# Sliding-window attention and a gated MLP on one core: some transposes of x moved from TensorE to DMA

## The chip, the core and the metric

The kernel runs on one NeuronCore of a Trainium2 chip. A core has TensorE (PE in the profile, with its weight loads as PEld), VectorE (DVE), ScalarE (ACT), GpSimd (POOL), SyncE (SP) and 16 DMA engines. Here SP and POOL do little more than issue DMAs. The metric is the device time of one execution in microseconds; lower is better. Executions differ by about half a per cent.

## What is computed

Eight batches of eight heads go through causal attention with a window of 128 and a distance penalty per head. The result, 4608 tokens of 512 features, goes through a two-layer MLP with the activation h cos h.

```python
scores = scale * np.matmul(q, k.transpose(0, 1, 3, 2))          # q, k, v: 8 x 8 x 576 x 64
mask = (rel >= 0) & (rel < window)                              # window = 128
scores = np.where(mask, scores + bias[None], -1000000000.0)     # bias = -slope_h * |rel|
attn = softmax(scores)
x = np.matmul(attn, v)            # to 4608 x 512
h = x @ w_in                      # 512 x 2048
g = h * np.cos(h)
out = g @ w_out                   # 2048 x 512
```

## The kernel before

**Units and chunks.** Attention is cut into 64 units. A batch has eight: one for its first 128 queries and all heads (`qb` 0, "first unit"), six for 128 queries and half of the heads each (`qb` 1 to 3, "half-width units"), and one for its last 64 queries and all heads (`qb` 4, "tail unit"). The MLP is cut into nine chunks of 512 tokens. The first projection of chunk c (`moe1`, line 731; line 756 for chunk 0) makes 16 blocks of 128 features, 4 matmuls each; ACT takes the cosine of each block (line 736) and DVE multiplies (line 740) into `gT`, of which there are two. The second projection (`moe2`, line 784) has 64 matmuls per chunk, whose results go through `ob` (four buffers) to HBM by a store on SP (line 796).

**Phases.** Seven units are done in a startup phase. Then follows, for each chunk c, `moe1` of c, an exp phase c with eight units (nine in phase 6), and `moe2` of c. Phases exist because ACT holds one function table at a time (exp or sine). The eight units of phase c are the tail of batch c, then the first unit and the six half-width units of batch c + 1. They are handled in pairs: scores of both units (line 541), two exps (line 568), masks on DVE (line 587), the product with v (PV, lines 603 to 617) and the normalization (lines 640 to 656), which leaves x with tokens on partitions in `xtail`, `xfirst` or `xnat`. Scores use the four PSUM banks `SB`; PV uses the two banks `UB`. A half-width unit takes one bank of `UB`, so both units of a pair fit; a first or tail unit takes both.

**Transposes of x.** `moe1` needs x with features on partitions (`xT`). Function `x_pe` (line 661) does this with PE transposes into the free part of the unit's `UB` banks (line 675 for first and tail units, four each; line 694 for half-width units, two each) and copies out of PSUM by ACT or DVE (lines 703, 704: two copies for a first unit, one for any other). Function `x_dma` (line 708) does it with one DMA transpose from SBUF to SBUF, issued on SP (line 718, and 714 for first and tail units). Line 826 chooses `x_dma` only for units that do not begin in the chunk that comes next.

**Transposes of q and k.** From batch 2 on, POOL loads q and k with a cast to `qnat` and `knat` (line 380), and SP turns them into `qt` and `kt` by DMA transposes (lines 389 and 392, two issues each). `qnat` and `knat` have one buffer each, so the next load waits until the transposes have read them. `qt` and `kt` have two buffers by parity of the batch: those of batch c + 2 can be written once the scores of the tail of batch c, in the first pair of phase c, are done, and are read by the first pair of phase c + 1. POOL issues in program order: v of the next batch, then q and k.

**Order of the work.** Class `Plan` records every operation with an estimated occupancy (`occ`) and latency (`lat`) and derives dependencies from what it reads and writes. `schedule` is a list scheduler over these estimates: at each step it takes the earliest operation, on PE by priority (PV 1, scores 2, `moe1` 5, `moe2` 6; lower first). It fixes the order of every engine's instructions and of SP's issues. At run time each engine goes through its list in that order and waits on semaphores. Lines 170 to 178 estimate when a DMA ends; line 165 doubles PE's occupancies before `COLD`.

Of the kernel before, what the change touches and what calls it, by code (L numbers as in the profile page):

```python
# [12 lines left out]
NPAIR = H // 2  # L13
# [5 lines left out]
CH = 512  # L19
# [15 lines left out]
class Plan:  # L35
# [3 lines left out]
    SWITCH = 110  # L39
    TABLE = 1330  # L40
    START = {"pe": 1300, "act": 750, "dve": 1050, "pool": 550, "sp": 750}
    COLD = 8000
    FILL = 107

    def __init__(self, nc, ctx):
# [2 lines left out]
        self.writer, self.readers = {}, {}  # L48
        self.lastdma, self.lastseq = {}, {}

    def op(self, eng, fn, r=(), w=(), dma=None, occ=100, lat=None, pri=5, mode=0, table=None):
        o = Op()
        o.seq = len(self.all)
        o.eng = (eng,) if isinstance(eng, str) else tuple(eng)
        o.fn, o.r, o.w, o.dma = fn, tuple(r), tuple(w), dma
        o.occ, o.lat, o.pri, o.mode, o.table = occ, occ if lat is None else lat, pri, mode, table
        preds = {}
        for k in o.r:
            if k in self.writer:
                preds[self.writer[k]] = DATA  # L60
        for k in o.w:
            if k in self.writer:
                preds[self.writer[k]] = DATA
            for d in self.readers.get(k, ()):
                preds.setdefault(d, WAR)
        if dma is not None and dma in self.lastdma:
            preds[self.lastdma[dma]] = DATA
        if eng == "pool":
            if eng in self.lastseq:
                preds.setdefault(self.lastseq[eng], ORDER)  # L70
            self.lastseq[eng] = o
        if dma is not None:
            self.lastdma[dma] = o
        o.preds, o.succs, o.npred = preds, [], len(preds)
        for d in preds:
            d.succs.append(o)
        for k in o.r:
            self.readers.setdefault(k, []).append(o)
        for k in o.w:
            self.writer[k], self.readers[k] = o, []  # L80
        self.all.append(o)
        return o
# [7 lines left out]
    def schedule(self, filler=None, fill=(0, 0)):  # L90
# [32 lines left out]
        while avail:  # L123
            phase = next((t for t in tables if left[t]), None)
            best = None
            for e in ENG:
                cand = []
                for o in avail:
                    if e not in o.eng or (o.table is not None and o.table != phase):
                        continue  # L130
                    at = reach(o, e)
                    st = max(free[e], at)
                    if e == "pe":
                        if o.mode != mode:
                            st += self.SWITCH
                        if at > free[e]:
                            st += 40
                    cand.append((st, o))
                if not cand:
                    continue  # L140
                if e == "pe":
                    st, o = pick_pe(cand)
                else:
                    soon = min(st for st, _ in cand)
                    st, o = min(((st, o) for st, o in cand if st <= soon + 40),
                                key=lambda c: (c[1].pri, c[1].seq))
                key = (st, o.pri, o.seq)
                if best is None or key < best[0]:
                    best = (key, e, o)
            (st, _, _), e, o = best  # L150
            avail.remove(o)
            if o.table is not None and o.table != table:
                st += self.TABLE
            if len(o.eng) > 1:
                o.fn, o.occ, o.lat = o.fn[e], o.occ[e], o.lat[e]
                o.eng = (e,)
            if e == "pe":
                while filler and mode == 0 and free[e] + self.FILL + 30 < st and (
                        fill[0] <= free[e] < fill[1]):
                    p = self.op("pe", filler, r=["zeros"], occ=self.FILL, lat=self.FILL + 100)  # L160
                    self.all.pop()
                    p.start, p.end = free[e], free[e] + self.FILL
                    free[e] += self.FILL
                    order.append(p)
                if st < self.COLD:
                    o.lat += o.occ
                    o.occ *= 2
            o.start = st
            free[e] = st + o.occ
            if o.dma is not None:  # L170
                if e == "sp" and o.dma[0] in "tx":
                    cross = max(cross, st + 2300) + o.lat
                    o.end = max(cross, st + o.occ + 1400) + 500
                elif e == "sp" and o.dma[0] == "s":
                    o.end = st + o.occ + 1800 + o.lat
                else:
                    wire = max(wire, st + (2300 if e == "pool" else 1400)) + o.lat
                    o.end = max(wire, st + o.occ + 1400) + 500
            else:
                o.end = st + o.lat  # L180
            if e == "pe":
                mode = o.mode
            if o.table is not None:
                table = o.table
                left[o.table] -= 1
            order.append(o)
            for s in o.succs:
                s.npred -= 1
                if s.npred == 0:
                    avail.append(s)  # L190
# [85 lines left out]
def bass_alibi_sliding__then__act_gcu_kernel(  # L276
# [8 lines left out]
    with ExitStack() as ctx:  # L285
# [96 lines left out]
                    src[b, :, 128 * t:128 * t + rows, :].rearrange("h p d -> p h d")))  # L382
            op("pool", fns, w=[("nat", which)], dma=f"ldn{which}", occ=4400, lat=5500)

        def dma_transposes(b):
            for which in ("q", "k"):
                t = tr[which][b % 2][:, :].rearrange("p (c k t) -> p c k t", c=NBLK, k=NPAIR)
                fns = [
                    lambda e, t=t, which=which: e.dma_start_transpose(
                        t[:, 0:4, :, :].rearrange("p c k t -> p (c k) t"),  # L390
                        nat[which][:, 0:4, :, :].rearrange("p c h d -> p (c h d)")),
                    lambda e, t=t, which=which: e.dma_start_transpose(
                        t[:, 4, :, 0:64],
                        nat[which][0:64, 4, :, :].rearrange("p h d -> p (h d)")),
                ]
                op("sp", fns, r=[("nat", which)] + ([("ktail", b % 2)] if which == "k" else []),
                   w=[("tr", which, b % 2)], dma=f"tr{which}{b % 2}", occ=2500, lat=6500)

        def load_w_in(f0, f1):
            op("pool", [lambda e: e.dma_start(  # L400
# [118 lines left out]
        def t_first(u):  # L519
            return S * u[0] + 128 * u[1]  # L520
# [185 lines left out]
                   occ={"act": 281, "dve": 320}, lat={"act": 384, "dve": 405}, pri=0)  # L706

        def x_dma(u, n):
            b, qb, hh = u
            t0 = t_first(u)  # L710
            if qb in (0, 4):
                m = 64 if qb else 128
                src_, key = (xtl[b % 2], ("xtl", b % 2)) if qb else (xfirst, "xfirst")
                op("sp", [lambda e: e.dma_start_transpose(xT[:, :, t0:t0 + m], src_[:, :])],
                   r=[key], w=xkeys(range(NPAIR), t0, m), dma=f"xt{b % 2}" if qb else "xf",
                   occ=1250, lat=500)
                return
            op("sp", [lambda e: e.dma_start_transpose(
                xT[:, 2 * hh:2 * hh + 2, t0:t0 + 128], xnat[n % NX][:, :])],
               r=[("xnat", n % NX)], w=xkeys(range(2 * hh, 2 * hh + 2), t0, 128), dma=f"x{n % NX}",  # L720
               occ=1250, lat=500)
# [78 lines left out]
        ucount = [0]  # L800

        def attention(us, phase):
            for g in range(0, len(us), 2):
                two = us[g:g + 2]
                if phase < 0:
# [13 lines left out]
                for set_ in sets:  # L819
                    pv(set_)  # L820
                    after = []
                    for u, ub in set_:
                        n = ucount[0]
                        ucount[0] += 1
                        norm(u, ub, n)
                        after.append((t_first(u) // CH > phase + 1, u, ub, n))
                    for by_dma, u, ub, n in after:
                        if by_dma:
                            x_dma(u, n)
                        else:  # L830
                            x_pe(u, ub, n)

        load_qk("q", q, 0, 0)
        load_qk("k", k, 0, 0)
# [28 lines left out]
        for c in range(NCH):  # L863
# [13 lines left out]
                    moe1(c, fc, (UB + SB)[fc % 6] if done < len(every) else  # L877
                         (UB + SB)[(16 * c + fc) % 6])
            n = QUOTA[c] if c < len(QUOTA) else 0
            attention(every[done:done + n], c)  # L880
            done += n
            while next_v < B and done >= 8 * (next_v - 1):
                load_v(next_v)
# [1 line left out]
            while next_t < B and done >= 8 * (next_t - 1):  # L885
                if next_t < 4:
                    tail_zero(next_t)
                dma_transposes(next_t)
                next_t += 1
                if next_t < B:  # L890
                    load_nat("q", q, next_t)
                    load_nat("k", k, next_t)
# [32 lines left out]
```

## Time and profile before

| what | value |
|---|---|
| median of 3 runs | 320.49 us (320.01 to 321.6) |
| profiled execution, its own time | 321.72 us |
| its span in the profile | 320.0 us |
| granted TensorE clock, mean | 0.994 |
| transposes of x on PE (lines 675 and 694) | 108 |
| DMA transposes into `xT` (lines 714 and 718) | 25 |
| DMA transposes of q and k (lines 389 and 392) | 24 |

The profile is of one execution. Its page gives the busy time of each engine and the chain of work that ended last, followed back from the end. In the rows of the timeline the columns are start in us, duration in us, engine, line, operation, what is written and read, shape and count; a bracket holds the idle time of the engine before the row and what ended it. Rows of one kind that follow each other are merged. A row for SPq is the issue of a DMA by SP, not its transfer. Matmuls are pipelined, so their durations overlap; the distance between starts is what one costs. A few per cent of the matmul records are missing; the weight loads (PEld) are counted in full. A row of a table by stretches gives the stretch, its length, then for each engine busy time and count, the granted TensorE clock, the mean number of busy DMA packets per DMA engine, and GB/s.

### The profile page before, as it was taken

Reading aid. Unit: us, or ns where it says so; the run is one execution under the profiler, and the core shown is the slowest. Engines: PE = TensorE matmul, PEld = TensorE weight load, DVE = VectorE, ACT = ScalarE, POOL = GpSimd, SP = SyncE. Lnnn points to the kernel's source line nnn. Section 1 sums busy time; section 2 is a strip of 40 time slices with the busy share of each in tenths; the row PEclk is TensorE's granted clock in tenths of the full one; section 3 lists DMA queues with packets and bytes.
Section 4 is the critical chain, followed back from the end, with each engine's and each line's share of the span. In section 5 each row is a group of like instructions: output and inputs, shape, how many; then the busy total and the mean of one; then the engine's idle time right before and its main releaser. Section 6 shows DMA issues by size and latency. Waiting matters only on the chain.

```text
span 320.0 us, 6788 instructions
## 1 busy us (share of the span) xinstructions
PE 307.2 (96%) x2741; PEld 163.0 (51%) x2781; DVE 196.9 (62%) x424; ACT 203.4 (64%) x277; POOL 96.6 (30%) x124
## 2 busy tenths in 40 slices
PE   7499999999999999999999999999999999999996
PEld 4379855444554554445445544554455444444444
DVE  6289858486868686859785877766578542263000
ACT  6498767686778676866687768567668643263111
POOL 8789340084491076107613570100000000000000
PEclk9799999999999999999999999999999999999999
DMA  7999999999999399949998997971011200201112
GB/s 120 167 204 206 206 164 190 164 148 159 164 200 109 74 158 160 97 104 121 173 107 125 196 136 53 158 137 25 33 68 28 65 3 33 96 5 66 66 68 98
DMA packets 141663, 37.22 MB, mean 116 GB/s; under 512 B 130240, under 2 KB 136640, under 8 KB 141632
## 3 DMA queue, kind: packets, MB, share of 16 engines
q0 software_dynamic: 100144, 18.10, 76.8%
q1 hardware_dynamic: 41488, 18.69, 27.0%
q8 instruction: 22, 0.36, 0.5%
q14 instruction: 9, 0.07, 0.1%
HBM read 36.70 MB, written 9.44 MB: 144 GB/s over the span
## 4 chain that ended last, share of the span: by engine, by line
PE 90%; ACT 3%; DMA 2%; issue 2%; POOL 1%; DVE 1%; ACTq 0%; POOLq 0%
PE ps L784 39%; PE ps L731 32%; PE ps L541 5%; PE ps L756 4%; DMA qrows<-in_q_dram 2%; PE ps L615 2%; PE ps L617 2%; ACT p L568 2%; PE ps L483 1%; PE ps L675 1%; PE ps L603 1%; PE ps L694 1%; DVE gT L740 1%; ACT cos L736 1%; PE ps L607 1%
## 5 line engine op out<-in xcount | busy, mean ns | idle before, releaser
L784 PE MATMUL ps<-w_outb,gT 128*128 128x512 bf16 (+2 forms) x566 | 133.2, 373 | 2.4 <-issue 1.6
L731 PE MATMUL ps<-xT,w_inb 128*128 128x512 bf16 x499 | 113.2, 379 | 0.7
L740 DVE TENSOR_TENSOR gT<-ps,cos 128x512 bf16<-128x512 f32 x128 | 83.6, 687 | 45.8 <-PE ps L784 28.6
L736 ACT ACTIVATE cos<-ps,halfpi 128x512 f32<-128x512 f32 x128 | 83.2, 687 | 31.6 <-PE ps L731 16.6
L784 PEld LDWEIGHTS ps<-w_outb,gT 128*128 128x128 bf16 x592 | 53.5, 98 | 55.4
L568 ACT ACTIVATE p<-ps 128x1024 bf16<-128x1024 f32 x64 | 62.0, 1021 | 30.4 <-PE ps L541 30.3
L731 PEld LDWEIGHTS ps<-xT,w_inb 128*128 128x128 bf16 x512 | 48.9, 98 | 59.1 <-DVE gT L740 3.5
L370 POOL DMA_DIRECT2D vp<-in_v_dram x40 | 34.0, 880 | 68.4 <-PE ps L607 60.2
L587 DVE TENSOR_TENSOR p<-p,emask 128x1024 bf16<-128x1024 bf16 x61 | 41.0, 684 | 6.4 <-ACT p L568 6.2
L791 ACT ACTIVATE ob<-ps 128x512 f32<-128x512 f32 (+2 forms) x25 | 14.5, 581 | 36.8 <-PE ps L784 36.8
L380 POOL DMA_DIRECT2D qnat<-in_q_dram x30 | 25.3, 886 | 21.2 <-DMA qt<-qnat 21.2
L380 POOL DMA_DIRECT2D knat<-in_k_dram x30 | 25.4, 884 | 13.5 <-DMA kt<-knat 12.8
L541 PE MATMUL ps<-qt,kt 64*128 64x128 bf16 (+1 forms) x576 | 20.8, 212 | 0.4 <-ACT kt L497 0.4
L541 PEld LDWEIGHTS ps<-qt,kt 64*128 64x128 bf16 x576 | 14.7, 95 | 7.7 <-issue 3.2
L654 DVE TENSOR_TENSOR xnat<-ps,rec 128x256 bf16<-128x256 f32 x48 | 18.3, 419 | 0.1
L756 PE MATMUL ps<-xT,w_inb 128*128 128x128 bf16 x256 | 16.8, 219 | 0.2 <-DVE rec L652 0.2
L615 PEld LDWEIGHTS ps<-vp,p 128*128 128x128 bf16 x192 | 12.7, 97 | 7.2 <-issue 6.4
L615 PE MATMUL ps<-vp,p 128*128 128x65 bf16 x192 | 15.2, 193 | 0.3
L617 PE MATMUL ps<-vp,p 128*128 128x65 bf16 x192 | 15.2, 193 | 0.0
L756 PEld LDWEIGHTS ps<-xT,w_inb 128*128 128x128 bf16 x256 | 14.5, 98 | 0.9 <-issue 0.3
L792 DVE COPY ob<-ps 128x512 f32<-128x512 f32 x12 | 8.3, 688 | 9.3 <-PE ps L784 9.2
L617 PEld LDWEIGHTS ps<-vp,p 128*128 128x128 bf16 x192 | 12.5, 97 | 0.0
(63 smaller groups left out, 173.3 us busy)
## 6 DMA issues: line engine op xcount, KB each, us to landing
out_dram<-ob SPq DMA_DIRECT2D x35, 256.0 KB, 2.3
vp<-in_v_dram POOLq DMA_DIRECT2D x32, 128.0 KB, 6.9
qnat<-in_q_dram POOLq DMA_DIRECT2D x24, 128.0 KB, 7.0
knat<-in_k_dram POOLq DMA_DIRECT2D x24, 128.0 KB, 6.3
w_outb<-in_moe_w_out_dram POOLq DMA_DIRECT2D x4, 512.0 KB, 19.8
w_inb<-in_moe_w_in_dram POOLq DMA_DIRECT2D x3, 512.0 KB, 13.0
qrows<-in_q_dram POOLq DMA_DIRECT2D x1, 576.0 KB, 12.8
krows<-in_k_dram POOLq DMA_DIRECT2D x1, 576.0 KB, 15.6
```

The source lines that it names most:

```text
L370: op("pool", [lambda e, t=t, rows=rows: e.dma_start(vp[b % 2][0:rows, t, :, 0:64], v[b, :, 128 * t:128 * t + rows, :].rearrange("h p d -> ...
L380: fns.append(lambda e, t=t, rows=rows: e.dma_start(nat[which][0:rows, t, :, :], src[b, :, 128 * t:128 * t + rows, :].rearrange("h p d -> p ...
L541: ins = e.matmul(ps[:, banks[x], c0:c0 + n_], keys_ap(b, x, pr, kc), query_ap(b, x, pr, qb, n_), start=not acc, stop=stop)
L568: op("act", lambda e: e.activation(P[i][:, 0:1024], ps[:, banks[0]:banks[0] + 2, :].rearrange("p a b -> p (a b)"), ACTF.Exp, scale=0.125), ...
L587: op("dve", lambda e: e.tensor_tensor(p, p, m, ALU.mult), r=[("P", i), ("EM", 0), ("EM", 1)], w=[("P", i)], occ=600, lat=690, pri=1)
L615: e.matmul(o, P[i][:, c0:c0 + 128], V[:, qb - 1, h, 0:65], start=True, stop=False)
L617: ins = e.matmul(o, P[i][:, c0 + 128:c0 + 256], V[:, qb, h, 0:65], start=False, stop=True)
L731: op("pe", lambda e, kc=kc: e.matmul(ps[:, bank, :], w_in[:, kc, 128 * fc:128 * fc + 128], xT[:, kc, r0:r0 + CH], start=(kc == 0), stop=(k ...
L736: op("act", lambda e: e.activation(cosb[ci][:, :], ps[:, bank, :], ACTF.Sin, bias=halfpi[:, 0:1]), r=["halfpi"], w=[("B", bank), ("cos", c ...
L740: op("dve", lambda e: e.tensor_tensor(gT[gi][:, fc, :], ps[:, bank, :], cosb[ci][:, :], ALU.mult), r=[("cos", ci)], w=[("B", bank)] + [("g ...
L756: ins = e.matmul(ps[:, bank, 128 * i:128 * i + 128], w_in[:, kc, 128 * fc:128 * fc + 128], xT[:, kc, t0:t0 + 128], start=(kc == 0), stop=( ...
L784: op("pe", lambda e, t=t, fc=fc, bank=bank, j0=j0, j1=j1: e.matmul(ps[:, bank, 0:j1 - j0], gT[gi][:, fc, 128 * t:128 * t + 128], w_out[:, ...
```

## The change

In every exp phase the x of the first units goes by `x_dma` instead of `x_pe`: the first pair in phase 0, the first two pairs in phases 1 to 6 (a unit for which line 826 already chose `x_dma` stays there). The q and k transposes of the same phase are ordered behind these transfers on SP; this order is one of the plan, without a semaphore. Three estimates of the scheduler change: `COLD`, the delay of DMA transposes on SP before 200 us, and the occupancy of the q and k transposes.

```diff
-    COLD = 8000
+    COLD = 5400
...
-    def op(self, eng, fn, r=(), w=(), dma=None, occ=100, lat=None, pri=5, mode=0, table=None):
+    def op(self, eng, fn, r=(), w=(), dma=None, occ=100, lat=None, pri=5, mode=0, table=None,
+           after=()):
...
+        for d in after:
+            preds.setdefault(d, ORDER)
...
                 if e == "sp" and o.dma[0] in "tx":
-                    cross = max(cross, st + 2300) + o.lat
+                    cross = max(cross, st + (5200 if st < 200000 else 2300)) + o.lat
...
-        def dma_transposes(b):
+        def dma_transposes(b, after):
...
-                   w=[("tr", which, b % 2)], dma=f"tr{which}{b % 2}", occ=2500, lat=6500)
+                   w=[("tr", which, b % 2)], dma=f"tr{which}{b % 2}", occ=4500, lat=6500,
+                   after=after)
...
         def attention(us, phase):
+            begin = []
...
-                        after.append((t_first(u) // CH > phase + 1, u, ub, n))
-                    for by_dma, u, ub, n in after:
-                        if by_dma:
+                        soon = g < (4 if phase else 2) and phase >= 0
+                        after.append((soon, t_first(u) // CH > phase + 1, u, ub, n))
+                    for soon, late, u, ub, n in after:
+                        if soon:
+                            begin.append(x_dma(u, n))
+                        elif late:
                             x_dma(u, n)
                         else:
                             x_pe(u, ub, n)
+            return begin
...
-            attention(every[done:done + n], c)
+            begin = attention(every[done:done + n], c)
...
-                dma_transposes(next_t)
+                dma_transposes(next_t, begin)
```

`x_dma` itself is unchanged but for returning the operation that it records.

More of the change, by code (lines that the diff above doesn't have):

```diff
@@ L713, in x_dma @@
                 src_, key = (xtl[b % 2], ("xtl", b % 2)) if qb else (xfirst, "xfirst")
[L714 to L718, printed above, removed]
+                return op(
+                    "sp", [lambda e: e.dma_start_transpose(xT[:, :, t0:t0 + m], src_[:, :])],
+                    r=[key], w=xkeys(range(NPAIR), t0, m), dma=f"xt{b % 2}" if qb else "xf",
+                    occ=1250, lat=500)
+            return op("sp", [lambda e: e.dma_start_transpose(
                 xT[:, 2 * hh:2 * hh + 2, t0:t0 + 128], xnat[n % NX][:, :])],
```

## The prediction

> **What bounds the kernel now.** I read the page's busy shares and its chain first, then the timeline of TensorE (PE) in an exp phase, then stretches counted by line.
>
> ```profile
> PE 307.2 (96%) x2741; PEld 163.0 (51%) x2781; DVE 196.9 (62%) x424; ACT 203.4 (64%) x277; POOL 96.6 (30%) x124
> PE 90%; ACT 3%; DMA 2%; issue 2%; POOL 1%; DVE 1%; ACTq 0%; POOLq 0%
> ```
>
> PE is busy in 307.2 of 320.0 us and carries 90% of the chain; the other engines stay under two thirds. Busy PE alone does not prove a bound, so the next question is whether PE has other work whenever something is late. It does if matmuls of the second projection (line 784) are still owed when the first projection of the next chunk starts. The stretches below, of line 784 alone, end where each phase hands over to line 731 (59.3, 90.78, 122.7, 151.78 us). The weight loads in the second bracket count its matmuls, because some matmul records are missing.
>
> ```profile
> core 0: us, PE busy (x) PEld busy (x), PEclk, DMA share, GB/s
> 0.00:59.30 59.30, 14.81 (x59) 5.43 (x63) 0.97 1.50 178
> 59.30:90.78 31.48, 13.35 (x55) 4.88 (x56) 1.00 1.67 163
> 90.78:122.70 31.92, 13.26 (x53) 4.80 (x55) 1.00 1.42 133
> 122.70:151.78 29.08, 10.85 (x43) 3.90 (x45) 1.00 1.33 115
> ```
>
> Each chunk owes 64. Done by the four ends: 63, 119, 174, 219, of 64, 128, 192, 256. So 1, 9, 18 and 37 are left when chunks 1, 2, 3, 4 begin. One costs 0.216 us (5.18 / 24 below, a row of line 731 with the same 512 columns). The stock is 0.2, 1.9, 3.9 and 8.0 us: almost nothing in phase 0, ample from phase 3 on. PE is thus the bound, and time taken from it should show in the end.
>
> ```profile
> 258.97 5.18 PE ps L731 x24
> ```
>
> **The change: what leaves PE.** Each unit's transposes stand between matmuls of line 784, so their price is the end of the last matmul before (start plus 0.216 each) to the start of the next.
>
> ```profile
> 173.98 0.81 PE L784 MATMUL ps<-w_outb,gT 128*128 128x512 bf16 x3
> 174.72 0.29 PE L675 MATMUL ps<-ident,xtail 64*128 64x64 bf16 x4
> 174.94 0.60 PE L784 MATMUL ps<-w_outb,gT 128*128 128x512 bf16 x2
> ...
> 176.93 0.59 PE L784 MATMUL ps<-w_outb,gT 128*128 128x512 bf16 x2 [0.16 <-issue]
> 177.44 0.40 PE L675 MATMUL ps<-ident,xfirst 128*128 128x128 bf16 x4
> 177.68 0.59 PE L784 MATMUL ps<-w_outb,gT 128*128 128x512 bf16 x2
> ```
>
> ```profile
> 118.53 0.81 PE L784 MATMUL ps<-w_outb,gT 128*128 128x512 bf16 x3
> 119.21 0.28 PE L694 MATMUL ps<-ident,xnat 128*128 128x128 bf16 x2
> 119.34 0.38 PE L784 MATMUL ps<-w_outb,gT 128*128 128x512 bf16 x1
> ...
> 119.67 0.59 PE L784 MATMUL ps<-w_outb,gT 128*128 128x512 bf16 x2
> ```
>
> Tail unit: 174.94 - (173.98 + 3 x 0.216) = 0.31. First unit: 177.68 - (176.93 + 2 x 0.216) = 0.32. The two half-width units: 119.34 - (118.53 + 0.648) = 0.16 and 119.67 - (119.34 + 0.216) = 0.11, together 0.27. From the code, tail and first units of phases 0 to 6 move (7 each), and the half-width pair of phases 1 to 4 (in 5 and 6 it goes by DMA already). Sum: 7 x 0.31 + 7 x 0.32 + 4 x 0.27 = **5.5 us** off PE. The same gap around another tail looks wider:
>
> ```profile
> 111.94 1.04 PE L784 MATMUL ps<-w_outb,gT 128*128 128x512 bf16 x4
> 112.91 0.29 PE L675 MATMUL ps<-ident,xtail 64*128 64x64 bf16 x4
> 113.36 1.03 PE L784 MATMUL ps<-w_outb,gT 128*128 128x512 bf16 x4 [0.16 <-issue]
> ```
>
> 113.36 - (111.94 + 0.864) = 0.56. I take a missing matmul record there, which would restore 0.34; were it real for all seven, the sum would be 7.2, the upper end.
>
> The 29 copies out of PSUM (lines 703, 704: one, two, one, one per unit) leave ACT and DVE, off the path. They also free the two UB banks sooner. In phase 2:
>
> ```profile
> 114.06 0.68 DVE L587 TENSOR_TENSOR p<-p,emask 128x1024 bf16<-128x1024 bf16 x1
> 117.82 0.20 PE L615 MATMUL ps<-vp,p 128*128 128x65 bf16 x1
> 118.73 0.76 DVE L654 TENSOR_TENSOR xnat<-ps,rec 128x256 bf16<-128x256 f32 x2
> ```
>
> The probabilities of the second pair were masked by 114.74, its PV started only at 117.82: 3.1 us behind the first pair's transposes and copies. Without these, up to 3.1 us of earliness are available.
>
> **What is added: DMA transposes on SP.** 22 more, each with a landing time of the kind that 24 transposes have now:
>
> ```profile
> L718 SPq DMA_TRANSPOSE xT<-xnat x24: 1168/1216/2509, 92.4 to 250.1; - x24
> DMA to landing us min/median/max: 2.3/4.9/7.5
> ```
>
> Issuing takes 1.2 us on SP, landing 4.9 (2.3 to 7.5). A late landing would block line 731 at PE's head, for the order is fixed. Without any earliness, the second half-width unit of phase 2 is normalized at 119.49 and issued behind its sister at about 120.7; line 731 would start at 122.70 - 0.9 (0.31 + 0.32 + 0.27 saved) = 121.8. At 4.9 it lands at 125.6: 3.8 late against 3.9 of stock, cost nothing. In phase 1,
>
> ```profile
> 86.54 0.76 DVE L654 TENSOR_TENSOR xnat<-ps,rec 128x256 bf16<-128x256 f32 x2
> ```
>
> gives issue at 88.5, landing 93.4, need 89.9, 3.5 late against 1.9: 1.6 us. Phase 3 has 8 us of stock, and I take the later phases to be like it. In phase 0,
>
> ```profile
> 49.67 0.88 DVE L643 TENSOR_TENSOR xfirst<-ps,rec 128x256 bf16<-128x256 f32 x2
> ```
>
> the first unit is ready at 50.55 and needed at 59.3 - 0.6, 8.1 us on, over the slowest landing. So the cost lies between 0 (earliness in full) and 1.6; I take 0.3, nearer to 0, as 3.1 of earliness cover nearly all of 3.5. A rule of the Trainium skill bears on it: DMA: Bandwidth & Descriptors, "Two cost components", gives a transfer about 2.0 us fixed plus its bytes over 436 GB/s; that is an estimated 2.2 for 64 KB. The quiet minimum agrees, the median here does not, and the measurement decides; by the rule alone nothing would be late and the time would be 0.3 lower.
>
> **What is moved: q and k transposes.** Four issues per phase now start right after the first scores; they go behind the x transfers. Queued behind them on SP are the stores of line 796, on POOL the natural loads of q and k (which wait for these reads) and behind those the next v.
>
> ```profile
> 107.70 1.79 SPq L389 DMA_TRANSPOSE qt<-qnat  x1
> 112.01 3.02 SPq L389 DMA_TRANSPOSE kt<-knat  x1
> 122.61 4.21 POOL L380 DMA_DIRECT2D knat<-in_k_dram  x5 [4.99 <-DMA kt<-knat]
> 140.04 1.78 SPq L389 DMA_TRANSPOSE qt<-qnat  x1
> 153.73 6.31 SPq L718 DMA_TRANSPOSE xT<-xnat  x4
> 154.41 4.20 POOL L380 DMA_DIRECT2D knat<-in_k_dram  x5 [4.28 <-DMA kt<-knat]
> 139.39 0.56 PE ps L541 x24
> 168.64 0.58 PE ps L541 x24
> ```
>
> From the first q issue to the release by k: 122.61 - 107.70 = 14.9 and 154.41 - 140.04 = 14.4. Phase 2: new start 120.7 + 1.2 = 121.9, end 136.8, wanted by the scores at 139.39 - 0.9 = 138.5: hidden, by 1.7. The natural loads slide with it into a stretch where POOL has nothing. Stores wait up to the block of q and k issues; there are four ob buffers, 4 x 16 x 0.216 = 13.8 us of line 784 before one is reused. In phase 3 the margin is thinner (rival 2). The planner's constants (COLD, the transposes' price and delay) only reorder. COLD touches the first 8 us, and there
>
> ```profile
> 5.37 7.33 DMA qrows<-in_q_dram
> ```
>
> the load of q rows ends at 12.70, whatever PE did before: nothing.
>
> **Sum.** The profiled execution took 321.72 us (span 320.0): 321.72 - 5.5 + 0.3 = 316.5. It stands 1.23 above the median of 320.49, so on the median **315.3 us**.
>
> **Rivals.** (1) *x lands late.* At the slowest 7.5, without earliness: phase 2 lands 128.2, 6.4 late, less 3.9 is 2.5; phase 1 lands 96.0, 6.1 late, less 1.9 is 4.2. Together 6.7: 320.49 - 5.5 + 6.7 = 321.7, no change; half of it 318.3. For: landings of 7 occur beside POOL's loads. Against: q and k no longer go ahead.
>
> (2) *q and k become the wait, slower.* In phases 3 and 4 four x transfers of the later units can slip between q and k: 6.31 us of SP in the row at 153.73. The second pair of phase 3 is ready at 151.17:
>
> ```profile
> 150.41 0.76 DVE L654 TENSOR_TENSOR xnat<-ps,rec 128x256 bf16<-128x256 f32 x2
> ```
>
> Issues at 151.2 and 152.4, q from 153.6, k's end at 153.6 + 14.4 + 6.3 = 174.3, wanted at 168.64 - 0.9 = 167.7: 6.6 late, less half the earliness (1.5) 5.1, in two phases 10.2: 320.49 - 5.5 + 10.2 = 325.2. It decides from 2.75 us per phase on. Against: a planner that foresees it spends 29 to 37 owed matmuls (6 to 8 us) there.
>
> (3) *Nothing is gained.* If scores, exp, mask and PV paced the phases, the freed slots would stay empty: 320.5. For: the 3.1 us above. Against: line 784 runs between all pieces.
>
> (4) *A stall slows the clock.* After the start's idle wait the granted clock is lower:
>
> ```profile
> 8.00:13.00 5.00, 1.06 (x22) 0.79 (x24) 1.06 (x3) 1.99 (x3) 4.43 (x6) 0.93 1.31 160
> 13.00:41.00 28.00, 26.98 (x480) 22.77 (x478) 22.09 (x44) 22.63 (x31) 19.30 (x24) 0.95 1.34 202
> ```
>
> (the column before the last two), 28 x 0.05 = 1.4 us lost. Two stalls as in rival 2 would add 2.8: 328.0. The Trainium skill (TensorE: Matmul & The Clock Gate, Part 1) says that about 3.4 us of idle halve the clock; the trace agrees in direction, with 0.93.
>
> **How the numbers follow.** Forecast 0.60 (its own range 313.3, with the 7.2, to 317.0), rival 1 0.17, rival 2 0.13, rival 3 0.07, rival 4 0.03. The range 313.0 to 321.5 leaves out rivals 2 and 4 and little else. A measurement here tells about 0.5% from no change, so faster means under 318.9, slower over 322.1. Faster: 0.60 + 0.09 of rival 1 = 0.69. Same: 0.07 of it and 0.06 of rival 3, 0.13. Slower: 0.13 + 0.03 and 0.02 of the edges, 0.18.
>
> **What would show it.** Right: lines 675 and 694 down by 56 and 16 matmuls, PE busy down by some 5 us with idle unchanged, 47 rather than 25 transposes into xT landing in 3 to 5 us, PV of the second pair about 3 us sooner in its phase, and k's release before the next first scores. Wrong: idle PE before line 731 with a DMA into xT as releaser (rival 1), before line 541 with kt (rival 2), in the phases behind DVE or ACT (rival 3), or a clock under 1.00 after 41 us (rival 4).

## The result and the profile after

The changed kernel took 317.28 us (median of 6, 316.21 to 318.0) against 321.11 (median of 6 beside it): a ratio of 0.9867, 95% interval 0.9841 to 0.9892, or some 4.3 us (3.5 to 5.1). The ratio is estimated from the single runs; it is not the quotient of the two medians, which lie 3.8 us apart. The profiled execution took 316.21 us, with a span of 314.5. Line numbers have moved: 541 is now 545 (scores), 615 is 619 (PV), 675 and 694 are 679 and 698 (transposes on PE), 731 is 736, 784 is 789, 714 and 718 are 720 and 723 (x by DMA), 389 and 392 are 392 and 395 (q, k), 380 is 383.

The page's busy time and chain by engine:

```profile
PE 302.7 (96%) x2671; PEld 160.3 (51%) x2711; DVE 192.5 (61%) x400; ACT 203.6 (65%) x272; POOL 96.8 (31%) x124
PE 89%; ACT 3%; DVE 2%; DMA 2%; issue 1%; POOL 1%; ACTq 0%; POOLq 0%
```

PE is still the bound, with 4.5 us less work: lines 679 and 698 have 4 and 32 transposes left of 60 and 48. The transposes of x by DMA, by line, then the time from issue to landing of all 47, and its median by kind:

```profile
L723 SPq DMA_TRANSPOSE xT<-xnat x32: 1167/1237/2767, 82.3 to 258.3; - x32
L720 SPq DMA_TRANSPOSE xT<-xtail x8: 1172/1190/1838, 45.2 to 259.6; - x8
L720 SPq DMA_TRANSPOSE xT<-xfirst x7: 1189/1192/1350, 48.5 to 248.4; - x7
DMA to landing us min/median/max: 2.3/2.8/7.9
xT<-xtail SPq DMA_TRANSPOSE x8, 6.6
xT<-xfirst SPq DMA_TRANSPOSE x7, 4.8
xT<-xnat SPq DMA_TRANSPOSE x32, 2.4
```

The median over all fell from 4.1 (25 transposes) to 2.8 though there are almost twice as many, but this is the doing of `xnat` alone, which went from 4.9 to 2.4. The tail and first units, all but one of them new here, land after 6.6 and 4.8. The slowest is the first unit of phase 0: issued at 48.49, it took 7.9 us and was there at 56.3, just as line 736 began (56.38). Phase 2 as an example, on PE and SP, with the first scores of the kernel before in the first row:

```profile
107.00 0.63 PE L541 MATMUL ps<-qt,kt 64*128 64x64 bf16 x24
104.81 0.63 PE L545 MATMUL ps<-qt,kt 64*128 64x64 bf16 x24
113.31 0.19 PE L619 MATMUL ps<-vp,p 128*128 128x65 bf16 x1
...
111.00 1.17 SPq L720 DMA_TRANSPOSE xT<-xtail  x1
113.19 1.19 SPq L720 DMA_TRANSPOSE xT<-xfirst  x1
114.67 4.06 SPq L723 DMA_TRANSPOSE xT<-xnat  x2
118.77 1.99 SPq L392 DMA_TRANSPOSE qt<-qnat  x1
```

PV of the second pair starts 8.5 us after the first scores (113.31 - 104.81); it was 10.8 (117.82 - 107.0). So 2.3 of the 3.1 us of earliness came, and q goes out behind the fourth x. In phase 3, where rival 2 was expected, the q and k issues, the release of POOL by k, and the next first scores:

```profile
153.14 1.76 SPq L392 DMA_TRANSPOSE qt<-qnat  x1
159.87 2.27 SPq L392 DMA_TRANSPOSE kt<-knat  x1
170.21 3.51 POOL L383 DMA_DIRECT2D knat<-in_k_dram  x4 [6.03 <-DMA kt<-knat]
172.58 0.56 PE ps L545 x24
```

k is there by 170.2, 2.4 us before the scores, which nothing held back at that point but their place in the fixed order. That place is later than before: the scores of phases 4 and 5 come 35.4 and 35.1 us after those of the phase before (29.3 and 29.3 in the kernel before). What PE does meanwhile is shown by line 789 in stretches that end at each handover to line 736:

```profile
core 0: us, PE busy (x) PEld busy (x), PEclk, DMA share, GB/s
0.00:56.38 56.38, 13.72 (x55) 5.08 (x59) 0.97 1.46 180
56.38:88.75 32.37, 14.19 (x58) 5.32 (x61) 1.00 1.78 154
88.75:121.09 32.34, 14.17 (x57) 5.22 (x60) 1.00 1.32 134
121.09:153.86 32.77, 14.62 (x61) 5.66 (x64) 1.00 1.37 135
153.86:189.35 35.49, 17.03 (x73) 6.84 (x76) 1.00 1.32 147
189.35:220.38 31.03, 13.05 (x53) 4.92 (x55) 1.00 1.35 132
```

Added up as before: 59, 120, 180, 244, 320, 375 of 64, 128, 192, 256, 320, 384. Owed are 5, 8, 12, 12, 0 and 9; before, the fourth figure was 37. The plan spent what is owed ahead of the late scores. And in phase 5, x of the first unit became a wait (SP above, PE below):

```profile
213.34 1.84 SPq L720 DMA_TRANSPOSE xT<-xtail  x1
215.92 1.19 SPq L720 DMA_TRANSPOSE xT<-xfirst  x1
...
219.39 0.38 PE L789 MATMUL ps<-w_outb,gT 128*128 128x512 bf16 x1
220.38 0.81 PE L736 MATMUL ps<-xT,w_inb 128*128 128x512 bf16 x3 [0.62 <-ACT p L572]
```

PE stands from 219.61 (219.39 + 0.216) to 220.38, 0.77 us. The bracket names ACT, but x of the first unit landed at 220.18, 4.26 after its issue, and x of the tail at 220.0, 6.6 after its own. The second profile of this kernel (`e11_change_again`, below) tells the two apart: there the exps end at 221.85 (219.91 + 1.94), after line 736 has started (221.79), and x of the first unit lands at 221.6. So x is the releaser. A plan that priced it at 2.3 + 1.0 us after 200 us had it landed at 219.2.

For the rest of the text, a phase's **remainder** is its length, from its first scores to those of the next phase (the last to the span's end), less 0.2158 us (5.18 / 24, as in the forecast) for each weight load of lines 736 and 789 in it: scores, PV, transposes and waits. For phase 5 after:

```profile
207.55:239.93 32.38, 13.76 (x57) 5.31 (x59) 1.00 0.99 123
```

the row gives 59 loads of line 789, and line 736 has 64: 32.38 - 123 x 0.2158 = 5.8.

| remainder, us, phases 0 to 6 | 0 | 1 | 2 | 3 | 4 | 5 | 6 | sum |
|---|---|---|---|---|---|---|---|---|
| before | 6.5 | 6.1 | 6.2 | 6.2 | 6.0 | 5.6 | 5.8 | 42.4 |
| changed | 5.9 | 5.4 | 5.6 | 5.1 | 5.3 | 5.8 | 5.3 | 38.4 |

The phases give 4.0 us. The two profiled spans differ by 5.5; the other 1.5 lie ahead of the first scores of phase 0 (41.1 and 39.6) and are taken up first.

### The profile page after: what moved, and what is told of

It reads as the page before. It is cut to its first block, busy times and chain, and to the rows that moved or that the text cites. A ratio compares the mean times of both kernels' runs of the same rounds, so it can differ in the third digit from the quotient of the medians.

```text
span 314.5 us, 6624 instructions
## 1 busy us (share of the span) xinstructions
PE 302.7 (96%) x2671; PEld 160.3 (51%) x2711; DVE 192.5 (61%) x400; ACT 203.6 (65%) x272; POOL 96.8 (31%) x124
## 4 chain that ended last, share of the span: by engine, by line
PE 89%; ACT 3%; DVE 2%; DMA 2%; issue 1%; POOL 1%; ACTq 0%; POOLq 0%
PE ps L789 39%; PE ps L736 33%; PE ps L545 5%; PE ps L761 4%; PE ps L619 2%; ACT p L572 2%; DMA qrows<-in_q_dram 2%; PE ps L621 2%; DVE gT L745 2%; PE ps L487 2%; PE ps L607 1%; ACT cos L741 1%; PE ps L698 1%; PE ps L611 1%; POOL vp L373 0%
## 5 line engine op out<-in xcount | busy, mean ns | idle before, releaser
L789 PE MATMUL ps<-w_outb,gT 128*128 128x512 bf16 (+2 forms) x563 | 131.2, 373 | 2.2 <-issue 1.3
L736 PE MATMUL ps<-xT,w_inb 128*128 128x512 bf16 x502 | 111.6, 379 | 1.1 <-ACT p L572 0.6
L745 DVE TENSOR_TENSOR gT<-ps,cos 128x512 bf16<-128x512 f32 x128 | 85.2, 689 | 37.4 <-ACT cos L741 30.4
L741 ACT ACTIVATE cos<-ps,halfpi 128x512 f32<-128x512 f32 x128 | 84.9, 687 | 27.6 <-PE ps L736 19.2
L736 PEld LDWEIGHTS ps<-xT,w_inb 128*128 128x128 bf16 x512 | 49.6, 98 | 60.8 <-issue 1.3
L761 PEld LDWEIGHTS ps<-xT,w_inb 128*128 128x128 bf16 x256 | 14.5, 98 | 1.4 <-DMA w_inb<-in_moe_w_in_dram 0.6
```

What stands on the lines that cost most here:

```text
L736: op("pe", lambda e, kc=kc: e.matmul(ps[:, bank, :], w_in[:, kc, 128 * fc:128 * fc + 128], xT[:, kc, r0:r0 + CH], start=(kc == 0), stop=(k ...
L741: op("act", lambda e: e.activation(cosb[ci][:, :], ps[:, bank, :], ACTF.Sin, bias=halfpi[:, 0:1]), r=["halfpi"], w=[("B", bank), ("cos", c ...
L745: op("dve", lambda e: e.tensor_tensor(gT[gi][:, fc, :], ps[:, bank, :], cosb[ci][:, :], ALU.mult), r=[("cos", ci)], w=[("B", bank)] + [("g ...
L761: ins = e.matmul(ps[:, bank, 128 * i:128 * i + 128], w_in[:, kc, 128 * fc:128 * fc + 128], xT[:, kc, t0:t0 + 128], start=(kc == 0), stop=( ...
L789: op("pe", lambda e, t=t, fc=fc, bank=bank, j0=j0, j1=j1: e.matmul(ps[:, bank, 0:j1 - j0], gT[gi][:, fc, 128 * t:128 * t + 128], w_out[:, ...
```

## The experiments

**The start.** Two runs ask whether `COLD` moved it.

```diff
-    COLD = 5400
+    COLD = 8000
```

> The changed kernel with the planner's constant COLD back at 8000. In the profiles the first scores of phase 0 came 1.5 us sooner after the change (39.58 against 41.10), which the forecast had put at nothing. Theory A (the start differs because the second load of q rows landed sooner in that one execution, 11.02 against 12.70; COLD does nothing): within 0.5 us of the changed kernel, 317.3. Rival B (COLD itself gives the 1.5): 318.8, with the first scores of phase 0 near 41.1 in the profile.

Measured: 316.62 us, ratio 0.9889 (0.9834 to 0.9944), first scores at 39.8. The time is 0.7 below the changed kernel's, more than the 0.5 expected, but inside its wide interval. The reverse, in the kernel before:

```diff
-    COLD = 8000
+    COLD = 5400
```

> The kernel before with COLD at 5400 alone. Theory A (landing of the q rows varies, COLD does nothing): as before, 321.1 within 0.5. Rival B (COLD gives 1.5): 319.6.

Measured: 320.98 us, ratio 0.9998 (0.998 to 1.0016). `COLD` does nothing that this run resolves: the rival's 1.5 us lie far outside its interval, which is about 0.6 us to each side. What varies is the load of q rows on which PE waits. Two executions of the changed kernel, the first the profiled one above, the second from a later run (`e11_change_again`, below); chain of waits, start and length:

```profile
5.57 5.45 DMA qrows<-in_q_dram
39.65 0.56 PE ps L545 x24
```

```profile
5.54 7.33 DMA qrows<-in_q_dram
41.32 0.56 PE ps L545 x24
```

The load takes 5.45 or 7.33 us in the same program, and the first scores move with it, by 1.7. The 1.5 us of the profiles are this, not the change.

**The transposes on PE taken away.**

```diff
                         if by_dma:
                             x_dma(u, n)
+                        elif phase >= 0 and g < (4 if phase else 2):
...
+                            op("dve", lambda e, p0=prs_[0], p1=prs_[-1] + 1, t_=t_, m_=m_: e.memset(
+                                xT[:, p0:p1, t_:t_ + m_], 0.0),
+                               r=[key_], w=xkeys(prs_, t_, m_), occ=280, lat=330, pri=0)
                         else:
                             x_pe(u, ub, n)
```

> The kernel before, in which the x of the units that the change moves is not transposed at all: VectorE writes zeros into their columns of xT in place of the PE transposes and the copies. Nothing is added to DMA and q and k stay where they were. Theory (each of the 72 transposes' slots on PE is worth what the gaps in the timeline say): 321.0 - 5.5 = 315.5. Rival (part of the freed slots stays empty, as pieces of the chain scores, exp, mask, PV show up behind them): 317 to 318, like the changed kernel.

Measured: 316.01 us, ratio 0.9837 (0.9809 to 0.9865), 5.2 us (4.3 to 6.1). The remainders sum to 37.42, 4.9 below the 42.36 of before. Such sums repeat closely: the run with `COLD` alone has 42.36 again. Removing the transposes is worth nearly the 5.5 of the working, and the interval reaches over it. The copies and their hold on UB are gone in this run too, and DVE writes zeros instead, so it prices the whole step and not the slots alone. The changed kernel lies about 1 us short of this.

**The move of q and k alone.**

```diff
                         norm(u, ub, n)
+                        if g < (4 if phase else 2) and phase >= 0:
+                            begin.append(R.all[-1])
...
-                        if soon:
-                            begin.append(x_dma(u, n))
-                        elif late:
+                        if late:
                             x_dma(u, n)
                         else:
                             x_pe(u, ub, n)
```

> The changed kernel, in which x is transposed on PE as before, and the q and k transposes are ordered behind the normalizations of the same units. Only the move of q and k (and the planner's estimates) is left. Theory (the move is hidden, k lands before the next first scores): as before, 321.0 within 1. Rival (the move costs by itself, for the plan takes k to land late and spends owed matmuls ahead of the scores): 322 to 323.

Measured: 321.56 us, ratio 1.0015 (0.9991 to 1.0038). The move is hidden, as forecast. The stock does shrink: 38 matmuls are owed at the handover of phase 5, where the kernel before owes 77, and enough is left that it costs nothing.

**The order of q and k taken away.**

```diff
-                dma_transposes(next_t, begin)
+                dma_transposes(next_t, ())
```

> The changed kernel without the order of the q and k transposes behind the x transfers: they go out as soon as the first scores are done. Theory (the order is needed because x would land behind q and k): the four q and k issues hold SP for about 8 us, x of the second pair is issued some 3 us later and lands in 6 to 7 us instead of 2.3 to 5.5, so line 736 waits 1 to 3 us in phases 0 to 2, where little of the second projection is owed: 319 to 322, with idle PE before line 736 ended by a DMA into xT. Rival (owed matmuls cover it, the order is worth nothing): 317.3 within 0.5.

Measured: 328.98 us, ratio 1.0268 (1.0227 to 1.0308): slower than even the theory's upper end. The remainders sum to 50.7 against 38.4; 8.6 of this is in phase 1, most of the rest in phases 2 to 4, and no second projection is owed at any handover from phase 1 to 5. Phase 1 on SP, and PE around the wait:

```profile
73.19 5.18 SPq L392 DMA_TRANSPOSE qt<-qnat  x1
78.41 1.42 SPq L395 DMA_TRANSPOSE qt<-qnat  x1
...
80.50 1.33 SPq L720 DMA_TRANSPOSE xT<-xtail  x1
83.39 5.55 SPq L392 DMA_TRANSPOSE kt<-knat  x1
88.98 1.94 SPq L395 DMA_TRANSPOSE kt<-knat  x1
90.97 1.26 SPq L720 DMA_TRANSPOSE xT<-xfirst  x1
```

```profile
89.81 1.24 PE L789 MATMUL ps<-w_outb,gT 128*128 128x512 bf16 x5
98.10 1.46 PE L736 MATMUL ps<-xT,w_inb 128*128 128x512 bf16 x3 [7.05 <-DMA xT<-xnat]
```

The issue of k takes 5.55 us on SP, then 1.94, and x of the first unit waits behind it until 90.97. PE stands 7.05 us. The rest of that phase's loss is the clock (line 736 in stretches; the third column from the end is the granted clock):

```profile
91.00:94.50 3.50, 0.00 (x0) 0.00 (x0) 0.94 2.20 179
94.50:98.00 3.50, 0.00 (x0) 0.00 (x0) 0.50 1.64 199
98.00:101.50 3.50, 3.40 (x10) 1.30 (x11) 0.58 1.74 163
101.50:105.00 3.50, 3.45 (x17) 1.60 (x17) 1.00 1.99 215
```

At 0.58 for 3.5 us, some 1.5 us more are lost after the wait has ended. Phase 1's remainder is 14.0 against 5.4: 7.05 + 1.5 make up 8.5 of the 8.6.

**The wait in phase 5.**

```diff
-                    cross = max(cross, st + (5200 if st < 200000 else 2300)) + o.lat
+                    cross = max(cross, st + 5200) + o.lat
```

> The changed kernel with the planner's delay of 5200 for DMA transposes in the whole run, not only before 200 us. Theory (in phase 5 PE stood 0.8 us before line 736 until x of the first unit landed, because the plan took it for landed after 3.3 us and it took 4.3 to 6.6): the wait goes, 0.5 to 0.8 us faster than the changed kernel, 316.6. Rival (what is owed by then is spent, the idle time only moves): 317.3 within 0.3.

Measured: 318.21 us, ratio 0.9916 (0.9888 to 0.9944): the rival, or worse. Phase 5's remainder falls to 5.4, phase 6's rises from 5.3 to 7.4. Phase 5 in the stretches of line 789, and PE in phase 6:

```profile
207.12:241.90 34.78, 16.55 (x70) 6.51 (x72) 1.00 1.03 122
```

```profile
254.06 0.41 PE L545 MATMUL ps<-qt,kt 64*128 64x64 bf16 x16
256.13 0.19 PE L619 MATMUL ps<-vp,p 128*128 128x65 bf16 x1 [1.66 <-DVE p L591]
```

Phase 5 now takes 72 matmuls of line 789 where it took 59. The 13 are missing in phase 6, where PE waits 1.66 us for a mask: with nothing owed, the chain of scores, exp, mask and PV shows through. What is owed covers one wait, not two.

**Other estimates for q and k.**

```diff
-                    cross = max(cross, st + (5200 if st < 200000 else 2300)) + o.lat
+                    cross = max(cross, st + (5200 if o.dma[0] == "x" else 2300)) + o.lat
```

> The changed kernel with other estimates in the plan: DMA transposes of x take 5200 from issue in the whole run, those of q and k 2300 as before the change. Theory (the scores of phases 4 and 5 were planned about 3 us after k had landed, and the matmuls spent ahead of them are missing in phases 5 and 6): the scores come sooner, PE's time outside the MLP matmuls falls to about 5.3 us in phase 5 without rising in phase 6, 0.5 to 1 us faster than the changed kernel, 316.2. Rival (k then lands after the scores are wanted): a wait before line 545 with kt as releaser, 318 or more.

Measured: 316.26 us, ratio 0.9841 (0.9808 to 0.9874): the time of the theory, but not beside the changed kernel. Beside it on one chip, both again:

> The kernel with the 5200 for x in the whole run and 2300 for q and k, once more beside the changed kernel. Theory (owed matmuls are no longer spent ahead of late planned scores, so the wait for x in phase 5 goes and none comes in phase 6): 0.8 us below the changed kernel, 0.984 of before. Rival (its 316.26 was a difference of chips): within 0.3 us of the changed kernel.

> The changed kernel as it is, beside the next one on one chip, to narrow its ratio. Theory (5.2 us of freed slots less about 1 us of waits in phases 5 and before): 0.987 of before. Rival (the first measurement had the lucky starts): 0.990 or more.

Measured: 316.95 us (0.9869, 0.9845 to 0.9892) and, as it is, 317.24 us (0.9874, 0.9839 to 0.9908). They lie 0.3 apart, which is the rival's outcome. The traces show the wait of phase 5 gone and none new: remainders of 5.3 and 5.4 in phases 5 and 6 in both runs, a sum of 37.7 against 38.1 for the changed kernel beside it. These 0.4 us are below what the runs resolve. The premise was half right: the scores of phase 4 came 34.5 us after those of phase 3, only 0.9 sooner.

**Half-width units back on PE.**

```diff
-                        soon = g < (4 if phase else 2) and phase >= 0
+                        soon = g < 2 and phase >= 0
```

> The changed kernel with the first pair alone by DMA in every phase (tail and first units); the half-width units of phases 1 to 4 are back on PE. Theory (16 transposes return, 4 x 0.27): 1.1 us slower than the changed kernel, 318.1. Rival (these were not on the bound: their x came late as often as it freed PE): 317.0 within 0.5.

Measured: 317.93 us, ratio 0.9883 (0.9856 to 0.991), 3.8 us below before, so only some 0.5 above the changed kernel. In the remainders phases 1 to 4 rise by 0.24, 0.27, 0.13 and 0.43 against the first profile of the changed kernel, 1.1 in all as the slots say, and phase 5 falls from 5.8 to 5.45, where 59 matmuls are owed at the handover in place of 9. That both happen at once fits the stock; the difference of the medians does not prove it.

**One pair more by DMA.** To the kernel with the other estimates:

```diff
-                        soon = g < (4 if phase else 2) and phase >= 0
+                        soon = g < (6 if phase in (1, 2) else 4 if phase else 2) and phase >= 0
...
-                            begin.append(x_dma(u, n))
+                            o = x_dma(u, n)
+                            if g < 4:
+                                begin.append(o)
```

> The kernel with the 5200 for x and 2300 for q and k, and in phases 1 and 2 the third pair of units by DMA too (8 more transposes off PE). Theory (the slot is worth 0.27 per pair, and what is owed then covers the landing): 0.5 us below the kernel without it, 315.7. Rival (x of the third pair is wanted by line 736 about 3 us after its normalization, less than it takes to land, and in phases 1 and 2 next to nothing is owed): 1 to 3 us above it, with idle PE ahead of line 736.

Measured: 325.7 us, ratio 1.0135 (1.01 to 1.017), 8.8 above the kernel without it (316.95): the rival, and more than its 3 us. Phase 1 on SP and PE, then the clock:

```profile
88.06 1.67 SPq L395 DMA_TRANSPOSE qt<-qnat  x1
89.77 5.11 SPq L723 DMA_TRANSPOSE xT<-xnat  x4
```

```profile
89.63 1.03 PE L789 MATMUL ps<-w_outb,gT 128*128 128x512 bf16 x4
92.30 0.81 PE L736 MATMUL ps<-xT,w_inb 128*128 128x512 bf16 x3 [1.65 <-issue]
94.45 1.86 PE L736 MATMUL ps<-xT,w_inb 128*128 128x512 bf16 x4 [1.34 <-DMA xT<-xnat]
```

```profile
90.60:94.50 3.90, 0.86 (x4) 0.30 (x5) 0.87 0.74 76
94.50:98.00 3.50, 3.50 (x9) 1.23 (x10) 0.50 1.96 135
98.00:102.00 4.00, 4.00 (x15) 1.52 (x13) 0.71 1.42 201
```

x of the third pair goes out behind q and lands when PE has nothing left. The two waits are 3.0 us; the clock at 0.50 and 0.71 costs 3.50 x 0.50 + 4.00 x 0.29 = 2.9 more. The phase's remainder is 11.45 against 5.4, phase 2's 7.8.

## Why the prediction was right

The forecast was 315.3 on a median of 320.49, 5.2 us faster. The measured gain is 4.3 (3.5 to 5.1), and 4.0 in the second comparison (3.0 to 5.2).

**PE is the bound, and the slots are its price.** Shown: without the transposes and with only zeros written by DVE in their place, 5.2 us go (4.9 by the remainders), against a sum of 5.5. By the recorded durations (0.29, 0.40 and 0.28 in the rows of the forecast) the sum would have been 7.1. The upper end of 7.2, from the wide gap around one tail, is out: its interval ends at 6.1, which fits the missing matmul record.

**UB free sooner.** Right in direction, 2.3 of 3.1 us in phase 2. No run took this part away by itself.

**x lands in time in phases 1 to 4.** Right. The second half-width unit of phase 2 is issued at 117.5 and lands at 119.9, 1.2 us before the handover at 121.09. The tail and first units land no faster than forecast (6.6 and 4.8 against 4.9), so they are in time because they are issued early. For phase 0 the forecast saw room over the slowest landing; with 7.9 us and 56.3 against 56.38 there was none, and that nothing was lost there is luck. The rule that the forecast took from the Trainium skill (DMA: Bandwidth & Descriptors, "Two cost components") is fitted there to transfers that GpSimd issues; of the transposes, which SP issues, only the quickest (2.3 us) come near its 2.2. The condition that x goes ahead of q and k is shown by the run without the order: rival 1 came true there and cost more than the 6.7 us worked out for it.

**The added wait of 0.3 us: the term that was mis-sized.** The step was "Phase 3 has 8 us of stock, and I take the later phases to be like it". The stock was read from the kernel before, and the change spends it: at the handovers of phases 3 to 5 it is 12, 0 and 9 matmuls in place of 37 and more. So phase 5 has a wait of 0.77 us that the sum lacks. By the remainders the change lies 1.0 us above the run without transposes (38.40 and 37.42; 0.7 in its second profile, 38.13), where the sum had 0.3. Half of that is phase 5, 5.83 against 5.33. Phases 0 to 3 have 0.1 to 0.2 more each, and phases 4 and 6 slightly less; the cause of this part stays open. By these measures the gain was forecast too large in both terms, the slots (5.5, not 4.9 to 5.2) and the wait (0.3, not 0.7 to 1.0), and the two errors add. A further 0.6 of the miss on 315.3 is the median of before, which was 320.49 then and is 321.11 with the later runs.

**q and k behind x.** Right: hidden in time, 1.0015 alone, and in the changed kernel's trace line 545 never waits for a transposed k. Rival 2 said that a planner which foresees the lateness spends owed matmuls; this happened, at no price where it was spent and with the consequence above where it was missing.

**COLD.** Right, nothing. The profiles alone would have misled here, as 1.5 us of their difference are the landing of the first loads.

**The clock (rival 4).** Not in the changed kernel, whose waits are under 0.8 us, but shown twice in the runs that had longer ones.

## What to carry to other kernels

Where one engine is full, price a step by the gap that it leaves between its neighbours on that engine, not by its recorded duration (here 5.5 against 7.1, and 5.2 measured). Before counting on spare work to cover a new wait, ask whether the change, or the plan that it alters, spends that work earlier: the same 13 matmuls cover one wait or another, not both. In this kernel a DMA transpose was a good exchange for PE time only with its order on the issuing queue settled: the order was worth about 12 us, more than the move itself.

## What the runs showed of the hardware

The issue of a large DMA transpose (line 392) held SP from 1.4 to 5.5 us within one execution of the changed kernel, so its issue time is not a constant; no run isolates what sets it. In the run with a third pair, a mean clock of 0.87 over the 3.90 us from 90.60, with 0.50 in the next stretch, means that the granted clock fell to 0.50 at about 93.5. By then PE had stood for 1.65 us, worked for 0.81 and stood for 0.4 more, and the slow stretch cost about as much (2.9 us) as the two waits (3.0). In the run without the order, 0.94 over the 3.50 us from 91.00 puts the fall at about 94.1, some 3.0 us after PE had stopped. The Trainium skill (TensorE: Matmul & The Clock Gate, Part 1) states about 3.4 us of idle for it, which is near the second case and not the first, where neither wait was that long. The landing of the same first load varied from 5.45 to 7.33 us between two executions of the changed kernel and moved the first scores of phase 0 by 1.7 us.
